# Written order on every engine, and the second read of each batch as float32 products in four column tiles

## The chip, the cores and the metric

The kernel runs on one core of one Trainium2 chip. The metric is the device time of one execution in microseconds (us), as the median of several runs; lower is better. A profile of one execution gives the start and length of every instruction on the five engines: PE (TensorE, the matrix products; its weight loads stand apart as PEld), DVE (VectorE), ACT (ScalarE), POOL (GpSimd) and SP (SyncE, which here only issues DMAs).

## What is computed

```python
# x: 8 batches, 8 heads, 512 tokens, 64; state: 8, 8, 32, 64 (float32)
scores  = scale * x @ state^T            # first read: tokens look at the 32 states
a       = softmax(scores);   xread = a @ state
scores2 = scale * state @ x^T            # second read: the states look at the tokens
a2      = softmax(scores2);  sread = a2 @ x
y = concatenate([xread, sread], axis=2)  # 544 rows of 512 in each batch
h = maximum(y @ w_in, 0)                 # w_in: 512 x 2048
out = (h * h) @ w_out                    # w_out: 2048 x 512
```

The weights arrive as 64-bit floats and are turned into float32 on the chip. Most products are made of float32r halves: each operand is split into a high part (`hi`, a cast) and the rest (`lo`), and three products hi·hi, hi·lo and lo·hi stand for one.

## The kernel before

**Blocks.** The 4352 rows of the output are worked through in nine blocks: block b (0 to 7) holds the 512 token rows of batch b, block 8 the 256 state rows of all batches. In a block the 2048 hidden columns are cut in 16 chunks `fc`. `hidden.b.fc` makes one chunk: 6 products (12 of half the width in block 8) into the PSUM tile `ph`, then relu, square, the cast to `g_hi` and the rest `g_lo`. `accumulate.b.fc` multiplies it with chunk fc of `w_out`: three products for each of the four 128-row tiles `acc`, so 12 (6 in block 8). On PE the chunks stand as hidden.k+1 ahead of accumulate.k, so that the work after the products of chunk k has the time of accumulate.k-1 and hidden.k+1. Blocks 0 and 1 are interleaved in halves (0.0–0.7, 1.0–1.7, 0.8–0.15, 1.8–1.15), since the weights are still arriving: `decode_wi` and `prep_wo` turn them into float32 (one operation on ACT, four on DVE, L353 to L362), `split_wo` splits them. Half of block 0 uses plain float32 products (L644, L685).

**Ahead of each block, for its batch** (`class Attention`, L382): `prep` transposes x into `xT`; `scores` makes both score matrices by products of 64x32 tiles, eight side by side on PE (`by_head`, L337); `transposed_scores`, `softmax` and `split_k` make the first read's weights as `k_hi`, `k_lo`; `make_w2` (L573) multiplies state with `w_in` in the same 64x32 tiles, so that `hidden` needs one product chain (four times per block, w2.b.0 to w2.b.6). For the second read, `exp_s` makes the exponentials `e2` (ACT, L467), `transposes` turns them by PE, and `sread` multiplies them with x: all four heads of a group g at once, of which the diagonal quarter is used. From batch 2 on both operands are split into halves (`split_n`, L513, and L531), which makes 12 products of 128x128 by 256 columns for each g; in batches 0 and 1 it is four float32 products (L540), which PE runs as two instructions each.

**PSUM.** `acc` has four banks, `ph` two, and one tile of two banks (`banks`, L296) is used in turn by scores, w2, transposes and sread: each must be read out in full before the next is written.

**Order.** `PLAN` (L29) lists the steps; a step is a generator, `~name` runs it to its next `yield`, `name` to its end. `keep_order` (L269) ties every instruction to the one before it on its engine while `pinned` holds. At the word `loose` (behind accumulate.0.15) it stops: from there the scheduler of the tile framework orders each engine's instructions, with high priority for the products of `by_head`. Block 8 stands between blocks 6 and 7.

**Who does what.** `SECOND` names the exceptions from the usual engine: `pick(key, first, second)` (L306) takes the second engine for a name listed there. The rests of splits and the two softmax operations on whole tiles (L482, L494) are done on POOL from batch 2 on, and so is `split_wi` (L618) for block 8. Squares: in block 0 and the first half of block 1 by ACT (relu, square, cast: L670, L671, L676); otherwise ACT relu, DVE multiply (L675), ACT cast; then DVE makes `g_lo` (L678).

Of the kernel before, what the change touches and what calls it, by code (L numbers as in the profile page):

```python
# [28 lines left out]
PLAN = """  # L29
# [12 lines left out]
    ~prep_wo.2 ~decode_wi.4 w2.0.1 split_wo.0 ~hidden.0.2 ~prep_wo.2 ~prep_wo.3 ~decode_wi.4 prep_wo.2 ~decode_wi.4
    ~transposes.0.0
    hidden.0.2 ~decode_wi.5 accumulate.0.1 decode_wi.4 transposes.0.0 ~decode_wi.5 load_wo.12 ~prep_wo.3
    ~decode_wi.7 ~decode_wi.5 ~prep_wo.3 decode_wi.5 ~prep_wo.3 ~decode_wi.8 load_wo.13 ~sread.0.0 ~decode_wi.6
    ~split_wo.1 prep_wo.3 split_wo.1 ~hidden.0.3 ~sread.0.0 ~decode_wi.6 ~decode_wi.7 ~decode_wi.6 ~prep_wo.4
    sread.0.0 ~w2.0.2 decode_wi.6
    hidden.0.3 ~prep_wo.4 load_wo.14 accumulate.0.2 ~decode_wi.7 ~prep_wo.4 w2.0.2 ~decode_wi.7 ~decode_wi.9
    ~prep_wo.4 decode_wi.7 prep_wo.4 ~prep_wo.8 load_wo.15 ~decode_wi.8 ~prep.1.0 ~split_wo.2 ~decode_wi.9
    ~decode_wi.8 ~hidden.0.4 split_wo.2 prep.1.0 ~decode_wi.8 ~prep_wo.5 prep.1.1 ~decode_wi.9 decode_wi.8 ~prep.1.2  # L50
    hidden.0.4 ~prep_wo.5 load_raw.10 ~decode_wi.9 accumulate.0.3 prep.1.2 ~prep_wo.5 decode_wi.9 ~prep_wo.9
    prep.1.3 ~prep_wo.5 load_raw.11 ~prep_wo.10 ~prep_wo.8 prep_wo.5 ~prep_wo.8 ~prep_wo.9 ~transposes.0.1
    ~split_wo.3 ~prep_wo.8 ~hidden.0.5 transposes.0.1 split_wo.3 prep_wo.8 ~prep_wo.6 ~prep_wo.9 ~sread.0.1
    ~split_wo.8 ~prep_wo.6 ~prep_wo.9
    hidden.0.5 ~prep_wo.6 split_wo.8 accumulate.0.4 ~sread.0.1 ~prep_wo.6 prep_wo.9 ~decode_wi.10 sread.0.1
    prep_wo.6 start.2 ~split_wo.9 load_p.2.0 ~decode_wi.10 split_wo.9 ~decode_wi.10 ~w2.0.3 ~decode_wi.11
    ~prep_wo.10 load_p.2.1 ~decode_wi.10 ~split_wo.4 ~decode_wi.11 w2.0.3 split_wo.4 scores.1 decode_wi.10
    ~prep_wo.7 load_p.2.2 ~decode_wi.11 ~prep_wo.7 ~hidden.0.6 transposed_scores.1.0 transposed_scores.1.1
# [6 lines left out]
    ~hidden.1.0 ~decode_wi.11 ~accumulate.0.7 ~prep_wo.10 decode_wi.11 transposes.1.0
    hidden.1.0 load_raw.13 ~prep_wo.10 prep.2.0 prep_wo.10 ~sread.1.0 accumulate.0.7 prep.2.1 prep.2.2 prep.2.3
    ~sread.1.0 ~hidden.1.1 ~split_wo.7 sread.1.0 ~w2.1.2 ~hidden.1.1 split_wo.7 accumulate.1.0 ~w2.1.2
    hidden.1.1 ~split_wo.10 w2.1.2 ~hidden.1.2 split_wo.10 ~transposes.1.1 ~hidden.1.2 accumulate.1.1 transposes.1.1
    hidden.1.2 ~decode_wi.12 ~decode_wi.13 ~decode_wi.12 ~sread.1.1 ~decode_wi.12 ~prep_wo.11 ~decode_wi.13
    ~decode_wi.12 ~decode_wi.13 ~hidden.1.3 ~sread.1.1 decode_wi.12 ~decode_wi.13 load_raw.14 ~prep_wo.12 sread.1.1  # L70
    accumulate.1.2 decode_wi.13 ~hidden.1.3 ~prep_wo.11 load_raw.15 ~prep_wo.12 ~prep_wo.11 ~prep_wo.12 ~prep_wo.13
    ~prep_wo.11 ~w2.0.4
    hidden.1.3 prep_wo.11 ~hidden.1.4 ~w2.0.4 ~prep_wo.12 ~prep_wo.13 ~split_wo.11 w2.0.4 accumulate.1.3 ~hidden.1.4
    split_wo.11 prep_wo.12 ~decode_wi.14
    hidden.1.4 ~hidden.1.5 ~split_wo.12 ~decode_wi.14 ~prep_wo.13 split_wo.12 ~hidden.1.5 accumulate.1.4
    ~decode_wi.14 ~prep_wo.13 ~decode_wi.14 prep_wo.13 ~decode_wi.15
    hidden.1.5 ~split_wo.13 ~hidden.1.6 decode_wi.14 ~decode_wi.15 split_wo.13 ~hidden.1.6 accumulate.1.5
    ~decode_wi.15 ~decode_wi.15 decode_wi.15 ~prep_wo.14
    hidden.1.6 ~prep_wo.15 ~prep_wo.14 ~hidden.1.7 ~prep_wo.14 ~prep_wo.15 ~prep_wo.14 ~hidden.1.7 accumulate.1.6
    ~prep_wo.15 prep_wo.14 ~prep_wo.15 ~split_wo.14 prep_wo.15  # L80
    hidden.1.7 ~split_wo.15 ~w2.0.6 split_wo.14 split_wo.15 ~hidden.0.8 ~w2.0.6 w2.0.6 ~hidden.0.8 ~accumulate.1.7
# [4 lines left out]
    hidden.0.12 ~hidden.0.13 ~hidden.0.13 accumulate.0.12
    hidden.0.13 ~hidden.0.14 ~hidden.0.14 accumulate.0.13
    hidden.0.14 ~hidden.0.15 ~hidden.0.15 accumulate.0.14
    hidden.0.15 accumulate.0.15 loose
    hidden.1.8 scores.2 load_n.2.0  # L90
    hidden.1.9 accumulate.1.8 transposed_scores.2.0 exp_s.2.0 w2.1.6
    hidden.1.10 accumulate.1.9 transposed_scores.2.1 exp_s.2.1 softmax.2.0
    hidden.1.11 accumulate.1.10 softmax.2.1 split_n.2.0 load_states.5
    hidden.1.12 accumulate.1.11 transposes.2.0 sread.2.0 split_n.2.1 prep_states.5
    hidden.1.13 accumulate.1.12 transposes.2.1 start.3 load_p.3.0 load_p.3.1 load_p.3.2 load_p.3.3 load_part.1
    hidden.1.14 accumulate.1.13 w2.2.0
    hidden.1.15 accumulate.1.14 sread.2.1
    hidden.2.0 accumulate.1.15 prep.3.0
    hidden.2.1 accumulate.2.0 prep.3.1 load_n.3.0 w2.2.2
    hidden.2.2 accumulate.2.1 prep.3.2  # L100
    hidden.2.3 accumulate.2.2 prep.3.3
    hidden.2.4 accumulate.2.3 scores.3
    hidden.2.5 accumulate.2.4 transposed_scores.3.0 exp_s.3.0 w2.2.4
    hidden.2.6 accumulate.2.5 transposed_scores.3.1 exp_s.3.1 softmax.3.0
    hidden.2.7 accumulate.2.6 softmax.3.1 split_n.3.0
    hidden.2.8 accumulate.2.7 transposes.3.0
    hidden.2.9 accumulate.2.8 sread.3.0 split_n.3.1 w2.2.6
    hidden.2.10 accumulate.2.9 transposes.3.1
    hidden.2.11 accumulate.2.10 sread.3.1
# [765 lines left out]
```

## Time and profile before

| what | value |
|---|---|
| time, median of 3 runs | 699.42 us (699.08 to 699.65) |
| the profiled execution | 697.38 us |
| its span in the profile | 695.6 us |
| granted PE clock, mean of the span | 0.989 |
| busy: PE, DVE, ACT, POOL | 670.2, 384.6, 322.8, 89.0 us |
| first product of hidden.0.0 | 24.4 us after the start of the span |
| first product of hidden.1.0 | 78.0 us |
| block 8 on PE | 576 to 622 us |
| last product | 691.4 us |

The time of a run holds the span and some 2 us around it. The span is the time from the first to the last instruction; the parts of the profile (busy times, waits, the chain of work that ended last, the timeline) are all of the one profiled execution. A product's own length in the profile (about 390 ns for 512 columns) includes its way through the array, so that the rate of PE is read from the distance between the starts of products.

### The profile page before, as it was taken

How to read it: one execution, taken by the hardware profiler on the slowest of the kernel's cores; microseconds unless marked ns; L12 is line 12 of the kernel's file. 1: busy time of each engine (PE TensorE's matmuls, PEld its weight loads, DVE VectorE, ACT ScalarE, POOL GpSimd, SP SyncE). 2: the span in 40 equal slices, each digit the busy share in tenths (PEclk: the TensorE clock that was granted, in tenths of full speed). 3: DMA queues.
4: the chain of work that ended last, by engine and by line, in shares of the span. 5: the costliest groups of instructions: out<-in, count | busy, mean ns of one | idle time of the engine just before them, and what ended most of it. 6: DMA issues, size and time to landing. Idle time of an engine off the chain costs nothing.

```text
span 695.6 us, 9267 instructions
## 1 busy us (share of the span) xinstructions
PE 670.2 (96%) x3488; PEld 505.9 (73%) x3488; DVE 384.6 (55%) x715; ACT 322.8 (46%) x607; POOL 89.0 (13%) x62
## 2 busy tenths in 40 slices
PE   3599899999999999999999999999999999999997
PEld 2254477768777877787777777778778778987886
DVE  4999979456467345734574445734473434235333
ACT  4476577563435334534453434543463444423322
POOL 0000000032104010401032100410050112400000
PEclk9799999999999999999999999999999999999999
DMA  9975154404231023102310232020010001001001
GB/s 284 394 235 125 50 161 90 132 1 133 60 97 25 1 61 61 61 0 61 62 61 0 61 52 71 0 49 13 1 60 5 12 15 61 1 1 32 0 1 60
DMA packets 84300, 46.21 MB, mean 66 GB/s; under 512 B 65056, under 2 KB 71712, under 8 KB 84256
## 3 DMA queue, kind: packets, MB, share of 16 engines
q1 hardware_dynamic: 82176, 45.10, 23.7%
q10 hardware_dynamic: 2080, 0.52, 0.4%
q8 instruction: 27, 0.44, 0.3%
q14 instruction: 17, 0.14, 0.1%
HBM read 34.08 MB, written 11.01 MB: 65 GB/s over the span
## 4 chain that ended last, share of the span: by engine, by line
PE 90%; DVE 7%; SPq 1%; issue 1%; DMA 1%; ACT 0%; DVEq 0%
PE acc L333 51%; PE ph L333 27%; PE w2ps L341 4%; PE pr L333 2%; PE acc L685 2%; PE ph L644 1%; PE pt L523 1%; PE sc L341 1%; PE pr L540 1%; DMA std<-in_state_dram 1%; DVE wi L362 1%; SPq L560 0%; DVE dec L359 0%; DVE deco L359 0%; DVE deco L362 0%
## 5 line engine op out<-in xcount | busy, mean ns | idle before, releaser
L333 PE MATMUL acc<-wo,g_hi 128*128 128x512 f32 x1024 | 288.8, 394 | 0.0
L333 PEld LDWEIGHTS acc<-wo,g_hi 128*128 128x128 f32 x1024 | 187.2, 188 | 57.6 <-ACT r L674 17.6
L675 DVE SCALAR_TENSOR_TENSOR ph<-ph,r 128x512 f32<-128x512 f32 (+1 forms) x120 | 79.5, 663 | 179.1 <-ACT r L674 179.1
L333 PE MATMUL ph<-k_hi,w 128*128 128x512 f32 x480 | 169.0, 393 | 2.1 <-DVE w L602 1.3
L333 PE MATMUL acc<-wo,g_lo 128*128 128x512 f32 x512 | 168.3, 392 | 0.0
L674 ACT ACTIVATE r<-ph 128x512 f32<-128x512 f32 (+1 forms) x120 | 68.3, 569 | 208.0 <-PE ph L333 207.9
L678 DVE TENSOR_TENSOR g_lo<-ph,g_hi 128x512 fp32r<-128x512 f32 (+1 forms) x136 | 89.2, 656 | 70.0 <-ACT g_hi L676 66.1
L333 PEld LDWEIGHTS acc<-wo,g_lo 128*128 128x128 f32 x512 | 95.6, 188 | 25.7 <-DVE s L492 3.4
L333 PEld LDWEIGHTS ph<-k_hi,w 128*128 128x128 f32 x480 | 90.4, 189 | 24.5 <-issue 2.5
L676 ACT CAST g_hi<-ph 128x512 fp32r<-128x512 f32 (+1 forms) x136 | 76.4, 562 | 66.0 <-DVE ph L675 65.1
L333 PE MATMUL ph<-k_lo,w 128*128 128x512 f32 x240 | 93.9, 391 | 0.0
L311 POOL TENSOR_TENSOR xs<-xn,xs 128x1024 fp32r<-128x1024 f32 x12 | 28.8, 2400 | 425.1 <-ACT xs L310 425.1
L333 PEld LDWEIGHTS ph<-k_lo,w 128*128 128x128 f32 x240 | 45.2, 188 | 9.1
L602 DVE TENSOR_TENSOR w<-w2ps,w 128x512 fp32r<-128x512 f32 x60 | 38.4, 682 | 8.2 <-ACT w L599 8.1
L341 PE MATMUL w2ps<-wi,stT 64*32 64x512 f32 (+1 forms) x544 | 36.8, 583 | 0.5 <-DVE wi L362 0.5
L599 ACT CAST w<-w2ps 128x512 fp32r<-128x512 f32 x60 | 32.4, 596 | 4.2 <-PE w2ps L341 4.2
L685 PE MATMUL acc<-deco,gf 128*128 128x512 f32 x64 | 29.2, 599 | 0.0
L311 POOL TENSOR_TENSOR s<-wi,s 128x1024 fp32r<-128x1024 f32 x8 | 19.2, 2403 | 73.6 <-ACT s L310 73.6
L548 ACT ACTIVATE srd<-pr,r 32x64 f32<-32x64 f32 x64 | 19.4, 304 | 16.0 <-PE pr L333 10.2
L644 PE MATMUL ph<-kf,w 128*128 128x512 f32 x32 | 17.3, 675 | 8.9 <-DVE kf L500 8.3
L333 PE MATMUL ph<-sr_k_hi,s 128*128 128x256 f32 x128 | 25.4, 282 | 0.0
L685 PEld LDWEIGHTS acc<-deco,gf 128*128 128x128 f32 x64 | 12.1, 195 | 13.5 <-issue 13.0
(79 smaller groups left out, 546.7 us busy)
## 6 DMA issues: line engine op xcount, KB each, us to landing
...
```

What stands on the lines that cost most here:

```text
L311: pick(key, PL, V).tensor_sub(lo, src, hi.bitcast(F32))
L333: m = T.matmul(ps, l, r, start=first and i == 0, stop=last and i == len(seq) - 1)
L341: m = T.matmul(ps, l, r, start=True, stop=True)
L548: A.mul(srd[q].rearrange("p e d -> p (e d)"), pr[q, j], r2[q])
L599: A.copy(w[:, u, g, 0], ps[g])
L602: V.tensor_sub(w[:, u, g, 1], ps[g], w[:, u, g, 0].bitcast(F32))
L644: T.matmul(ph, w[c][:, cs], k[c], start=c == 0, stop=c == G - 1)
L674: A.activation(r, ph, AF.Relu)
L675: V.scalar_tensor_tensor(ph, ph, 0.0, r, ALU.max, ALU.mult)
L676: A.copy(ghi, ph)
L678: V.tensor_sub(glo, ph, ghi.bitcast(F32))
L685: T.matmul(acc[i], ghi[:, ts(i, P)], wo[fc], start=first, stop=last)
```

## The change

Four things are changed.

1. `loose` goes, and with it `pinned`, the priorities and the pins in `mm3` and `by_head`: every engine keeps the written order to the end. The steady blocks 2 to 6 come from one template `BLOCK` (b is the block, n the batch behind it, whose attention is made meanwhile). Block 8 is last (`READS`), after block 7. The order of the first two blocks (`FIRST`) is written anew too: among others decode_wi.10 and 11, prep_wo.8 to 10 and split_wo.8 and 9 are later, and both groups of the transposes stand together.
2. `sread` makes one float32 product per head, group of 128 tokens and g: weights of 128x32, 64 columns, the four heads j into the four 32-row quarters of the output. `transposes` does both g at once, `split_n` and the split of the transposed exponentials go.
3. What POOL did in splits and softmax goes to DVE (`pick` has its engines swapped, `SECOND` loses those lists). Nearly all squares are made on ACT; the others (x.3, x.10, x.12 to x.15 and block 8) stay split between ACT and DVE.
4. The scaling of the second read is one ACT operation per g, in place of four; block 8 is stored with one DMA per tile, in place of four.

```diff
-    hidden.0.7 accumulate.0.6 exp_s.1.1 ~softmax.1.0 ~softmax.1.1 ~softmax.1.0 ~split_k.0.0 ~softmax.1.1
...
-    hidden.3.4 accumulate.3.3 scores.4
-    hidden.3.5 accumulate.3.4 transposed_scores.4.0 exp_s.4.0 w2.3.4
-    hidden.3.6 accumulate.3.5 transposed_scores.4.1 exp_s.4.1 softmax.4.0
...
+    hidden.0.6 ~softmax.1.0 ~softmax.1.1 ~exp_s.1.1 ~softmax.1.0 split_wo.4 ~softmax.1.1 exp_s.1.1 ~softmax.1.0
+    ~prep_wo.7 ~softmax.1.1 ~w2.1.0 ~split_wo.5 ~softmax.1.0 ~hidden.0.7 ~w2.1.0 ~softmax.1.1 ~prep_wo.6
+    ~softmax.1.1 ~softmax.1.0 ~prep_wo.6
+    hidden.0.7 softmax.1.0 ~softmax.1.1 ~split_k.0.0 prep_wo.6 ~softmax.1.1 split_k.0.0 accumulate.0.6 ~split_k.0.1
+    softmax.1.1 split_k.0.1 w2.1.0 ~prep_wo.7 ~transposes.1 ~split_wo.6 split_wo.5 ~prep_wo.7 ~hidden.1.0
...
+BLOCK = """
...
+    hidden.{b}.3 accumulate.{b}.2 scores.{n} ~hidden.{b}.4 ~hidden.{b}.4 transposed_scores.{n}.0
+    hidden.{b}.4 transposed_scores.{n}.1 ~exp_s.{n}.0 ~exp_s.{n}.1 accumulate.{b}.3 ~hidden.{b}.5 ~hidden.{b}.5
+    ~exp_s.{n}.0 ~exp_s.{n}.1 ~softmax.{n}.0
+    hidden.{b}.5 ~softmax.{n}.1 exp_s.{n}.0 exp_s.{n}.1 ~softmax.{n}.0 accumulate.{b}.4 ~w2.{b}.4 ~hidden.{b}.6
+    load_states.{s} start.{m} load_p.{m}.0 load_p.{m}.1 load_p.{m}.2 load_p.{m}.3 ~hidden.{b}.6 ~w2.{b}.4
+    ~softmax.{n}.0
...
+    hidden.{b}.10 softmax.{n}.1 accumulate.{b}.9 ~transposes.{n} ~hidden.{b}.11 ~hidden.{b}.11 transposes.{n}
+    hidden.{b}.11 accumulate.{b}.10 ~hidden.{b}.12 ~sread.{n} ~hidden.{b}.12 ~sread.{n}
+    hidden.{b}.12 sread.{n} prep_states.{s} accumulate.{b}.11 ~hidden.{b}.13 ~hidden.{b}.13
...
+    hidden.8.15 accumulate.8.14 accumulate.8.15
...
-            if i.engine in last and pinned[0]:
+            if i.engine in last:
...
     def split(hi, lo, src, key):
         A.copy(hi, src)
-        pick(key, PL, V).tensor_sub(lo, src, hi.bitcast(F32))
...
+        yield
+        pick(key, V, PL).tensor_sub(lo, src, hi.bitcast(F32))
...
-        def transposes(self, g):
-            b, e2 = self.b, self.e2.pop(g)
-            pt = banks(f"pt{b}_{g}")[:, 0].rearrange("p (k q) -> p k q", k=KC)
...
+        def transposes(self):
             b = self.b
+            t = banks(f"pt{b}")
+            for g in range(G):
+                e2 = self.e2.pop(g)
+                for k in range(KC):
+                    T.transpose(t[:, g, ts(k, P)], e2[:, k], ident)
+            yield
...
+                eT = p2.tile([P, G, S], F32, tag="wraw", name=f"eT{b}", bufs=RB)
+                evac(f"eT.{b}", eT, t)
...
-                hi, lo = self.xs.pop(g)
-                mm3(pr, [((eT[:, 0, k], eT[:, 1, k]), (hi[:, k], lo[:, k])) for k in range(KC)])
...
+            for g in range(G):
                 for k in range(KC):
+                    for j in range(NC):
+                        q = slice(32 * j, 32 * j + 32)
+                        xh = self.xn[:, k, 2 * j + g] if b < NX else self.xn[:, 2 * j + g, k]
+                        e = self.eT[g][:, P * k + 32 * j : P * k + 32 * j + 32]
+                        T.matmul(pr[q, g], e, xh, start=k == 0, stop=k == KC - 1)
+            yield
+            srd = p2.tile([P, G, D], F32, tag="srd", name=f"srd{b}", bufs=1)
+            for g in range(G):
+                A.mul(srd[:, g], pr[:, g], self.r2[g])
...
-                for j in range(4):
-                    SP.dma_start(out_v[4 * i + j, S : S + Ns], o[32 * j : 32 * j + 32])
+                pick(f"store.{i}", SP, A).dma_start(out_v[4 * i : 4 * i + 4, S : S + Ns], o)
```

More of the change, by code (lines that the diff above doesn't have):

```diff
@@ L42 @@
[L42 to L58, printed above, removed]
@@ L65 @@
[L65 to L81, printed above, removed]
@@ L82 @@
-    hidden.0.8 accumulate.1.7 load_states.2 ~hidden.0.9 ~hidden.0.9 accumulate.0.8
-    hidden.0.9 prep_states.2 ~hidden.0.10 load_part.0 ~hidden.0.10 accumulate.0.9
+    load_raw.6 ~prep.0.2 ~decode_wi.1 load_raw.7 prep.0.2 ~decode_wi.1 load_wo.5 ~prep.0.3 load_wo.6 ~prep_wo.0
+    decode_wi.1 load_wo.7 prep.0.3 ~prep_wo.0 ~w2.0.0 load_raw.8 ~prep_wo.0 load_raw.9 scores.0 w2.0.0 ~prep_wo.0
+    load_wo.8 load_wo.9 ~decode_wi.2 prep_wo.0 transposed_scores.0.0 ~decode_wi.3 transposed_scores.0.1 ~softmax.0.0
@@ new lines @@
+    start.1 ~prep_wo.1 load_n.1.0 ~softmax.0.1 ~softmax.0.0 load_n.1.1 ~softmax.0.1 ~softmax.0.0 ~exp_s.0.0
+    ~prep_wo.2 load_n.1.2 ~softmax.0.1 ~softmax.0.0 ~exp_s.0.0 ~softmax.0.1 load_n.1.3 ~softmax.0.0 ~decode_wi.4
+    ~softmax.0.1 ~softmax.0.0 ~softmax.0.1 softmax.0.0 softmax.0.1 exp_s.0.0 ~hidden.0.0 ~decode_wi.2 ~exp_s.0.1
+    ~decode_wi.2 ~exp_s.0.1 ~decode_wi.3 ~hidden.0.1 ~decode_wi.2
+    hidden.0.0 exp_s.0.1 decode_wi.2
+    hidden.0.1 accumulate.0.0 ~decode_wi.3 load_wo.10 ~prep_wo.1 ~decode_wi.3 ~decode_wi.5 ~prep_wo.1 decode_wi.3
@@ new lines @@
+    ~prep_wo.1 ~decode_wi.6 load_wo.11 ~prep_wo.2 ~w2.0.1 ~split_wo.0 prep_wo.1 w2.0.1 split_wo.0 ~prep_wo.2
+    ~hidden.0.2 ~prep_wo.3 ~decode_wi.4 ~prep_wo.2 ~decode_wi.4 ~transposes.0
+    hidden.0.2 prep_wo.2 ~decode_wi.4 accumulate.0.1 transposes.0 ~decode_wi.5 decode_wi.4 ~decode_wi.5 ~decode_wi.7
+    load_wo.12 ~prep_wo.3 ~decode_wi.5 ~prep_wo.3 decode_wi.5 ~sread.0 ~split_wo.1 ~prep_wo.3 load_wo.13
+    ~decode_wi.8 ~hidden.0.3 split_wo.1 ~sread.0 prep_wo.3 ~prep_wo.4 sread.0 ~prep_wo.4 ~w2.0.2 start.2
@@ new lines @@
+    hidden.0.3 load_p.2.0 ~decode_wi.6 accumulate.0.2 ~prep_wo.4 ~decode_wi.6 w2.0.2 ~prep_wo.4 load_p.2.1
+    ~decode_wi.6 prep_wo.4 decode_wi.6 load_p.2.2 ~prep.1.0 ~decode_wi.7 ~split_wo.2 ~decode_wi.8 ~decode_wi.9
+    split_wo.2 ~hidden.0.4 prep.1.0 ~decode_wi.7 ~decode_wi.8 load_p.2.3 ~decode_wi.7 ~prep_wo.5 prep.1.1 ~prep.1.2
+    ~decode_wi.8
+    hidden.0.4 decode_wi.7 accumulate.0.3 load_wo.14 ~prep_wo.5 prep.1.2 load_wo.15 decode_wi.8 ~prep_wo.5
+    ~prep_wo.8 load_raw.10 prep.1.3 ~decode_wi.9 ~prep_wo.9 ~prep_wo.5 ~decode_wi.9 ~w2.0.3 prep_wo.5 ~split_wo.3
@@ new lines @@
+    ~decode_wi.9 ~hidden.0.5 w2.0.3 split_wo.3 decode_wi.9 ~prep_wo.6 scores.1 ~prep_wo.8
+    hidden.0.5 load_raw.11 ~prep_wo.6 ~prep_wo.8 accumulate.0.4 transposed_scores.1.0 ~prep_wo.10
+    transposed_scores.1.1 ~exp_s.1.0 ~softmax.1.0 ~exp_s.1.0 ~softmax.1.1 ~hidden.0.6 ~split_wo.4 exp_s.1.0
+    ~softmax.1.0 ~exp_s.1.1 ~softmax.1.0 accumulate.0.5
+    hidden.0.6 ~softmax.1.0 ~softmax.1.1 ~exp_s.1.1 ~softmax.1.0 split_wo.4 ~softmax.1.1 exp_s.1.1 ~softmax.1.0
+    ~prep_wo.7 ~softmax.1.1 ~w2.1.0 ~split_wo.5 ~softmax.1.0 ~hidden.0.7 ~w2.1.0 ~softmax.1.1 ~prep_wo.6
@@ new lines @@
+    ~softmax.1.1 ~softmax.1.0 ~prep_wo.6
+    hidden.0.7 softmax.1.0 ~softmax.1.1 ~split_k.0.0 prep_wo.6 ~softmax.1.1 split_k.0.0 accumulate.0.6 ~split_k.0.1
+    softmax.1.1 split_k.0.1 w2.1.0 ~prep_wo.7 ~transposes.1 ~split_wo.6 split_wo.5 ~prep_wo.7 ~hidden.1.0
+    transposes.1 split_wo.6 ~prep_wo.7 ~sread.1 ~hidden.1.0 ~prep_wo.8 prep_wo.7 prep_wo.8 ~accumulate.0.7 ~sread.1
+    hidden.1.0 ~split_wo.8 sread.1 split_wo.8 load_n.2.0 ~prep_wo.9 ~decode_wi.10 ~prep_wo.10 ~decode_wi.10
+    ~prep_wo.9 ~w2.1.2 accumulate.0.7 ~decode_wi.10 ~prep_wo.9 ~decode_wi.10 prep_wo.9 ~w2.1.2 ~hidden.1.1
@@ new lines @@
+    decode_wi.10 ~prep_wo.10 load_raw.12 ~split_wo.7 w2.1.2 accumulate.1.0 ~hidden.1.1 split_wo.7 ~prep_wo.10
+    ~split_wo.9
+    hidden.1.1 ~hidden.1.2 split_wo.9 prep_wo.10 ~decode_wi.11 accumulate.1.1 prep.2.0 ~hidden.1.2 ~decode_wi.11
+    prep.2.1 ~decode_wi.11 ~split_wo.10
+    hidden.1.2 ~hidden.1.3 ~decode_wi.11 split_wo.10 ~hidden.1.3 accumulate.1.2 decode_wi.11 prep.2.2 load_raw.13
+    prep.2.3 ~decode_wi.12
+    hidden.1.3 start.3 load_p.3.0 ~prep_wo.11 ~w2.0.4 ~decode_wi.12 ~prep_wo.12 ~prep_wo.11 ~hidden.1.4
@@ new lines @@
+    ~decode_wi.12 ~w2.0.4 ~prep_wo.11 load_p.3.1 ~decode_wi.12 ~hidden.1.4 accumulate.1.3 w2.0.4 load_p.3.2
+    decode_wi.12
+    hidden.1.4 ~decode_wi.13 ~prep_wo.11 ~hidden.1.5 load_raw.14 ~decode_wi.13 prep_wo.11 load_p.3.3 ~hidden.1.5
+    accumulate.1.4 ~decode_wi.13 ~prep_wo.12 ~decode_wi.13 ~prep_wo.12 ~split_wo.11
+    hidden.1.5 decode_wi.13 ~hidden.1.6 split_wo.11 load_raw.15 ~prep_wo.12 ~decode_wi.14 accumulate.1.5 ~hidden.1.6
+    prep_wo.12 ~decode_wi.14 ~decode_wi.14 ~decode_wi.14 ~split_wo.12
@@ new lines @@
+    hidden.1.6 ~hidden.1.7 split_wo.12 decode_wi.14 ~decode_wi.15 accumulate.1.6 ~hidden.1.7 ~decode_wi.15
+    ~decode_wi.15 ~decode_wi.15 decode_wi.15 ~prep_wo.13 ~hidden.0.8
+    hidden.1.7 ~prep_wo.14 ~prep_wo.13 ~prep_wo.15 ~prep_wo.14 ~w2.0.6 ~hidden.0.8 ~prep_wo.13 ~prep_wo.14
+    ~accumulate.1.7 ~prep_wo.13 ~prep_wo.14 ~w2.0.6
+    hidden.0.8 prep_wo.13 w2.0.6 accumulate.1.7 prep_wo.14 ~prep_wo.15 ~prep_wo.15 ~split_wo.13 load_states.2
+    ~hidden.0.9 ~prep_wo.15 ~split_wo.14 split_wo.13 ~hidden.0.9 accumulate.0.8 split_wo.14 prep_wo.15 ~split_wo.15
@@ L84 @@
+    hidden.0.9 prep_states.2 ~hidden.0.10 split_wo.15 load_part.0 ~hidden.0.10 accumulate.0.9
     hidden.0.10 ~hidden.0.11 ~hidden.0.11 accumulate.0.10
     hidden.0.11 ~w2.1.4 ~hidden.0.12 ~w2.1.4 w2.1.4 ~hidden.0.12 accumulate.0.11
[L86 to L109, printed above, removed]
@@ L132 @@
-    hidden.4.2 accumulate.4.1 prep.5.2
-    hidden.4.3 accumulate.4.2 prep.5.3
-    hidden.4.4 accumulate.4.3 scores.5
-    hidden.4.5 accumulate.4.4 transposed_scores.5.0 exp_s.5.0 w2.4.4
-    hidden.4.6 accumulate.4.5 transposed_scores.5.1 exp_s.5.1 softmax.5.0
-    hidden.4.7 accumulate.4.6 softmax.5.1 split_n.5.0
-    hidden.4.8 accumulate.4.7 transposes.5.0
-    hidden.4.9 accumulate.4.8 sread.5.0 split_n.5.1 w2.4.6
-    hidden.4.10 accumulate.4.9 transposes.5.1
-    hidden.4.11 accumulate.4.10 sread.5.1
@@ L164 @@
-    hidden.6.2 accumulate.6.1 prep.7.2
-    hidden.6.3 accumulate.6.2 prep.7.3
-    hidden.6.4 accumulate.6.3 scores.7
-    hidden.6.5 accumulate.6.4 transposed_scores.7.0 exp_s.7.0 w2.6.4
-    hidden.6.6 accumulate.6.5 transposed_scores.7.1 exp_s.7.1 softmax.7.0
-    hidden.6.7 accumulate.6.6 softmax.7.1 split_n.7.0
-    hidden.6.8 accumulate.6.7 transposes.7.0
-    hidden.6.9 accumulate.6.8 sread.7.0 split_n.7.1 w2.6.6
-    hidden.6.10 accumulate.6.9 transposes.7.1
-    hidden.6.11 accumulate.6.10 sread.7.1
@@ L332, in mm3 @@
         for i, (l, r) in enumerate(seq):
-            m = T.matmul(ps, l, r, start=first and i == 0, stop=last and i == len(seq) - 1)
-            if pin and not pinned[0]:
-                tc.keep_in_program_order(m)
+            T.matmul(ps, l, r, start=first and i == 0, stop=last and i == len(seq) - 1)
     def by_head(jobs):
-        for i, (ps, l, r) in enumerate(jobs):
-            with tc.high_priority() if i and not pinned[0] else nullcontext():
-                m = T.matmul(ps, l, r, start=True, stop=True)
-            if i and not pinned[0]:
-                tc.keep_in_program_order(m)
+        for ps, l, r in jobs:
+            T.matmul(ps, l, r, start=True, stop=True)
     def decode(raw, shape, nm, out=None, tag="dec"):
@@ L679, in hidden, with accumulate @@
         return ghi, glo
-    def accumulate(acc, fc, g, nt, first, last, pin):
+    def accumulate(acc, fc, g, nt, first, last):
         ghi, glo = g
@@ L698, in store @@
         for i in range(nt // P):
-            if add is not None:
-                o = add[i]
+            o = p2.tile([P, DM], F32, tag="o", name=f"o{blk}_{i}", bufs=OB) if add is None else add[i]
+            if add is None:
+                evac(f"out.{blk}.{i}", o, acc[i])
+            else:
                 V.tensor_add(o, acc[i], o)
-            else:
-                o = p2.tile([P, DM], F32, tag="o", name=f"o{blk}_{i}", bufs=OB)
-                evac(f"out.{blk}.{i}", o, acc[i])
             if blk < B:
```

254 lines of the change are left out of this document (99 added, 155 removed).

## The prediction

> **What bounds the kernel now.** I read the page first: who is busy, at which clock, and which engine the chain of work that ended last runs through.
>
> ```profile
> span 695.6 us, 9267 instructions
> PE 670.2 (96%) x3488; PEld 505.9 (73%) x3488; DVE 384.6 (55%) x715; ACT 322.8 (46%) x607; POOL 89.0 (13%) x62
> ...
> PEclk9799999999999999999999999999999999999999
> ...
> PE 90%; DVE 7%; SPq 1%; issue 1%; DMA 1%; ACT 0%; DVEq 0%
> ```
>
> PE is busy for 96% of the span at nearly full clock, and 90% of the chain is PE. Busy is not yet dense, so the next views are the busy times by stretch, and the chain and timeline in a steady block.
>
> ```profile
> 24.43:62.50 38.07, 37.54 (x136) 18.51 (x136) 36.37 (x81) 24.66 (x48) 0.00 (x0) 0.94 0.77 249
> 62.50:82.00 19.50, 15.93 (x80) 6.75 (x80) 19.28 (x44) 11.79 (x23) 0.00 (x0) 0.95 0.33 68
> 82.00:104.00 22.00, 22.00 (x103) 15.95 (x101) 17.68 (x35) 15.65 (x32) 0.00 (x0) 0.97 0.53 140
> 104.00:131.00 27.00, 27.00 (x141) 20.66 (x141) 22.95 (x42) 19.02 (x34) 0.00 (x0) 1.00 0.41 104
> ...
> 430.00:506.00 76.00, 76.00 (x403) 58.35 (x401) 39.57 (x71) 34.12 (x63) 13.91 (x9) 1.00 0.10 29
> ```
>
> Columns: stretch, its length, then busy time of PE, weight loads, DVE, ACT and POOL. Up to 82 us DVE never rests (36.4 of 38.1, 19.3 of 19.5) and PE has holes; from 82 us on PE has none. In a steady block (430 to 506) DVE and ACT each work about half of the time. How dense PE is there, the chain tells, with start and length of each piece:
>
> ```profile
> 449.39 0.44 PE pt L523 x4
> 449.83 2.77 PE acc L333 x12
> 452.60 1.36 PE ph L333 x6
> 453.96 1.07 PE pr L333 x9
> 455.04 2.75 PE acc L333 x12
> 457.78 1.36 PE ph L333 x6
> 459.14 0.35 PE pr L333 x3
> ```
>
> Six products take 1.36 and twelve 2.72 to 2.77, so 227 ns each, back to back. In steady state time is saved only by taking work from PE, and every new wait of PE is paid in full.
>
> **The read that goes and the read that comes.** One old read of a group g costs 1.07 + 0.35 = 1.42, and the next accumulation 2.75 in place of 2.72: 1.45, so 2.9 us a batch for both groups. In batches 0 and 1 the chain has the float32 form, and below it stand the 64x32 tiles, whose float32 instructions run side by side:
>
> ```profile
> 40.69 1.74 PE pr L540 x8
> ```
> ```profile
> 429.03 0.39 PE L333 MATMUL ph<-k_hi,w 128*128 128x512 f32 x1
> ...
> 430.48 1.09 PE L341 MATMUL sc<-xT,stT 64*32 64x512 f32 x16
> 431.50 1.65 PE L333 MATMUL acc<-wo,g_hi 128*128 128x512 f32 x6
> 432.99 0.86 PE L333 MATMUL acc<-wo,g_lo 128*128 128x512 f32 x3
> ```
>
> Float32 over 256 columns takes 1.74 / 8 = 217 ns an instruction, the transposes' 128 columns 0.44 / 4 = 110; so 64 columns should take 55. The old form costs 2 x 1.74 = 3.5 us a batch. The sixteen instructions of scores on eight tiles take 1.02 (430.48 to 431.50): two rounds of 512 columns, each 2 x 217 = 0.43, so 0.86 of streaming. The switch of tile shape costs the rest: 0.16 there, 0.09 before (429.03 + 1.36 = 430.39, not 430.48) and 0.13 behind (six products take 1.49, not 1.36), together about 0.39.
>
> The new read has 2 groups x 4 k x 4 heads = 32 products, 64 instructions, 16 on each of four tiles. Side by side that is 16 x 0.055 = 0.88, plus 0.39: **1.27 us**. No row has a 128x32 tile. The bounds are 0.88 (switch free) and, all four tiles one after another, 64 x 0.055 + 0.39 = 3.9. I take 1.27, by the row it is nearest to: the 64x32 tiles differ only in that two row halves share the array.
>
> - Batches 2 to 7: 6 x (2.9 - 1.27) = -9.8.
> - Batches 0 and 1: 2 x (3.5 - 1.27) = -4.4.
> - The transposes of both groups share one entry: 0.44 + 0.05 behind them twice becomes 0.44 + 0.39 + 0.05, or 0.1 less: 6 x 0.1 = -0.6.
>
> The weight loads have to hide behind the products:
>
> ```profile
> 411.64 0.18 PEld L341 LDWEIGHTS w2ps<-wi,stT 64*32 64x32 f32 x16 [0.35 <-issue]
> ```
> ```profile
> L341 PEld LDWEIGHTS w2ps<-wi,stT 64*32 64x32 f32 x544 | 6.4, 105 | 15.0 <-issue 9.6 <-ACT wo L314 1.5 <-DVE wi L362 1.4
> ```
>
> A load takes 105 ns, yet sixteen, two for each tile, are done in 0.18, while the first products of 0.43 run: they overlap. The Trainium skill, "TensorE: Matmul & The Clock Gate", in "Part 3: Packing small matmuls — row/col tiling", says that a weight load overlaps running products only when its row group differs; four 128x32 tiles share all rows, so this speaks against the change. The trace does not bear it out strictly, since the second load for each tile was made while that very tile's first product ran. It returns below as a rival.
>
> **The start.** Waits of PE (those up to 24 us, for the first loads and the first softmax, are untouched and left out):
>
> ```profile
> PE sc L341 <- ACT w L326: 1.5, 1, 1.5
> PE ph L333 <- DVE w L602: 1.3, 1, 1.3
> PE ph L333 <- ACT w L599: 0.7, 1, 0.7
> PE ph L644 <- ACT w L326: 0.5, 1, 0.5
> PE w2ps L341 <- DVE wi L362: 0.5, 1, 0.5
> ```
>
> Together 4.5 us, and behind nearly all stands a full DVE. The new order puts DVE work behind hidden.1.0 that stood before it, priced by these rows:
>
> ```profile
> L362 DVE SCALAR_TENSOR_TENSOR deco<-wo_raw,deco 128x512 uint32<-128x512 uint32 x16 | 10.9, 683 | 0.1
> ...
> L316 DVE TENSOR_TENSOR wo<-deco,wo 128x512 fp32r<-128x512 f32 x16 | 10.9, 684 | 0.0
> ...
> L357 DVE TENSOR_SCALAR deco<-deco 128x512 uint32<-128x512 uint32 x16 | 6.7, 422 | 0.1
> ```
> A whole decode is 2 x 0.42 + 2 x 0.68 = 2.2. Later are decode_wi.10, prep_wo.9 (2.2 each), the last two operations of prep_wo.8 (1.4), two short ones each of decode_wi.11 and prep_wo.7 (0.8 each), one of prep_wo.10 (0.4), and three split_wo (2.1): 9.9 us. The holes of 4.5 can close. But the work comes back between hidden.1.0 and hidden.0.10, where DVE had 22.0 - 17.7 + 27.0 - 23.0 = 8.3 us free (82 to 131): it is nearly full there too, and some wait must come back. Bounds 0 and -4.5; I take **-3.0**.
>
> **The new wait.** I walked the template's order through one block with the trace's durations. Every use of the shared two-bank tile finds it free in time but one: w2.b.4 takes it from scores, whose last readers are the two exponentials on ACT, now written behind the relu, square and cast of hidden.b.5.
>
> ```profile
> 106.84 0.58 ACT L670 ACTIVATE ph<-ph 128x512 f32<-128x512 f32 x1
> 107.45 0.58 ACT L671 ACTIVATE ph<-ph 128x512 f32<-128x512 f32 x1
> 108.07 0.59 ACT L676 CAST g_hi<-ph 128x512 fp32r<-128x512 f32 x1
> ```
> ```profile
> 68.82 0.68 ACT L467 ACTIVATE e<-sc,nb 128x512 f32<-128x512 f32 x1
> 69.39 0.20 ACT L467 ACTIVATION_READ_ACCUMULATOR e<-sc,nb 128x1 f32 x1
> ```
> ```profile
> 685.94 0.39 PE L333 MATMUL ph<-k_hi,w 128*128 128x512 f32 x1
> ...
> 686.43 0.60 ACT L674 ACTIVATE r<-ph 128x512 f32<-128x512 f32 x1 [2.13 <-PE ph L333]
> ```
>
> Count from the end of scores on PE. hidden.4 (0.13 + 1.36), accumulate.3 (2.72) and hidden.5 (1.36) are through at 5.57; the last product ends 0.16 later and ACT starts 0.10 after that (686.33 to 686.43): 5.83. Relu, square and cast take 1.82 (106.84 to 108.66): 7.65. Two exponentials take 0.57 + 0.20 + 0.68 = 1.45: 9.10, and 0.1 for the hand-over: 9.2. PE has finished accumulate.4 at 8.29 and would switch at 8.38. It waits **0.8 us** in each of blocks 2 to 6: +4.1. Behind w2.b.4 stands all of PE. Bounds: 0, if the tile is free sooner, and 1.6, if ACT comes as late again.
>
> **What I cost at nothing.** POOL's work moves to DVE (two softmax operations and a rest for each g, 6 x 0.68 = 4.1 a batch), but ten squares of 0.7 leave DVE: still about half of the block. ACT gains ten operations of 0.58 and loses the two long casts of `split_n`. The chain behind a hidden chunk stays near 2.6 us (three on ACT, 1.82, then 0.7 on DVE) against accumulate and hidden, 2.72 + 1.36 = 4.08, as cover; without cover it would cost what it is late, 16 times a block. Copying both transposes takes ACT one operation of about 1.0; walked like the wait above, it ends 0.9 us before the read needs it. SP's loads stand half a block ahead of use. Block 8 moves as a whole, at the same cost. At the end its last chain (four operations on half the columns) has one accumulation of 1.36 as cover, where block 7 had 2.72: up to 1 us; with some edges at block changes I take **+0.5**.
>
> **Sum.** -9.8 - 4.4 - 0.6 - 3.0 + 4.1 + 0.5 = -13.2. The span goes from 695.6 to 682.4. The profiled execution took 697.4, 2.0 below the median of 699.4; the difference is set against the median: **686.2 us**.
>
> **The rivals.**
>
> - *Loads not hidden.* If each round waits for its load (105 ns) as well, a read costs 16 x (0.105 + 0.055) + 0.39 = 2.95, 1.68 more; eight reads add 13.4: 699.6, no change. This is how the skill's rule of row groups would act here. Against it: the sixteen loads in 0.18.
> - *One tile after another* (slower). If the four column tiles do not run side by side, as would also follow if the change did not place them apart, a read costs 3.9, and eight add 21: 707.3. It decides from a read of 1.27 + 13.2 / 8 = 2.9 us on. For it: no row has full-height narrow tiles; against it: the row of scores, where four column tiles of each half do run together.
> - *More waits of the written order.* The scheduler could put something else first; a fixed order cannot. If ACT is 1 us late at one more place in each of six blocks (the copy of the transposes has 0.9 to spare): 692.
> - *No wait at w2.b.4.* Then 682.1. Against it: the walk above, which uses nothing but rows.
>
> **How the numbers follow.** Forecast 0.62 (own range 682.5 to 690, by the start's bounds and half of the unknown wait), more waits 0.13, no wait 0.10, loads not hidden 0.09, one after another 0.06. From 680.5 to 694.5 holds all but the last two (0.15) and the ends of the others (about 0.05). A measurement here tells about 0.2%, 1.4 us, from no change. Faster is forecast, more waits and no wait: 0.84, a trifle off for the worst of the waits; loads not hidden lies on the line: same 0.06; slower 0.10.
>
> **What would show it.** In the profile after: `pr` rows of 128x32 with about 0.9 to 1.1 us from first start to the next product (right), 2.5 or 3.5 (a rival). PE waits on ACT at w2 of about 0.8, five times. hidden.1.0 before 76 us, not 78. POOL near 0, DVE over 0.9 busy up to some 120 us. A period of a block of about 74.6, not 75.5. Wrong it would be by a `pr` that takes 3 us, or by PE holes at other steps in each block.

## The result, and the profile after

The changed kernel takes 692.33 us (median of 4 runs, 691.66 to 692.75), the kernel before beside it 699.46: ratio 0.9898, 95% interval 0.9881 to 0.9915. It is faster by 7.1 us where 13.2 were forecast. Its profiled execution took 692.39 us and has a span of 690.6, 5.0 less than before; the profiled execution of before lay 2 us below its median. One run of those reported below, 839.79 us at a granted clock of 0.749 where the nine others of its kernel (POOL's rests, in "DVE in the start") had 0.986 to 0.996, is left out of that kernel's median.

The page of the changed kernel, with busy times of the engines:

```profile
span 690.6 us, 9688 instructions
...
PE 655.5 (95%) x3824; PEld 488.1 (71%) x3824; DVE 363.4 (53%) x671; ACT 331.6 (48%) x609; POOL 0.7 (0%) x6
...
PEclk9999999999999999999999999999999999999998
```

PE has 15 us less to do, yet its share falls from 96 to 95%: two thirds of what was taken from PE did not come off the span. The timeline of PE shows the new read in a steady block:

```profile
248.26 0.39 PE L280 MATMUL ph<-k_hi,w 128*128 128x512 f32 x1
248.58 1.10 PE L483 MATMUL pr<-xn,eT 128*32 128x64 f32 x64
249.61 0.73 PE L280 MATMUL acc<-wo,g_hi 128*128 128x512 f32 x2
```

PE runs the 32 products as 64 instructions, and all 64 are through in 1.03 us (248.58 to 249.61). With 0.09 before (the product ahead ends its 0.23 at 248.26 + 0.23 = 248.49) and 0.13 behind (two products in 0.58, not 0.45, at 250.19) a read costs 1.25 us; 1.27 was forecast. So the expected gain is there, and the loss is elsewhere. Three places in time divide the span: the first product of hidden.0.10, the last product, the end.

Before, in PE's timeline:

```profile
131.04 0.39 PE L333 MATMUL ph<-k_hi,w 128*128 128x512 f32 x1
```

After, in the same view:

```profile
124.82 0.39 PE L280 MATMUL ph<-k_hi,w 128*128 128x512 f32 x1
...
680.34 0.40 PE L280 MATMUL acc<-wo,g_lo 128*128 128x512 f32 x1
```

The busy times of the last stretch, from the last product to the end (length, then PE, weight loads, DVE, ACT, POOL, clock, DMA share, GB/s), before:

```profile
691.39:695.60 4.21, 0.39 (x2) 0.00 (x0) 0.69 (x1) 0.34 (x1) 0.00 (x0) 0.86 0.64 237
```

and after:

```profile
680.34:690.60 10.26, 0.40 (x2) 0.00 (x0) 0.69 (x1) 0.33 (x1) 0.00 (x0) 0.68 0.17 51
```

| stretch | before | after | difference | forecast |
|---|---|---|---|---|
| to hidden.0.10 | 131.0 | 124.8 | -6.2 | -7.4 |
| to the last product | 560.4 | 555.5 | -4.8 | -6.3 |
| to the end | 4.2 | 10.3 | +6.1 | +0.5, with the last chain |

The last product comes 11 us earlier than before; 6 of them are given back after it, while only the last copies and stores run. Over this stretch the DMAs move 51 GB/s in the mean, for two stores of 256 KB; before it was 237, for four. The waits of PE after:

```profile
PE w2ps L285 <- ACT e L409: 2.7, 5, 0.5
PE acc L618 <- DVE deco L304: 2.4, 2, 1.8
PE pr L483 <- ACT eT L273: 1.1, 1, 1.1
PE w2ps L285 <- DVE wi L304: 0.7, 1, 0.7
```

The first is the forecast wait of w2.b.4, five times. The third was not forecast. Of these places the experiments asked.

### The profile page after: what moved, and what is told of

It is laid out like the page before. It is cut to its first block, busy times and chain, and to the rows that moved or that the text cites. A ratio compares the mean times of both kernels' runs of the same rounds, so it can differ in the third digit from the quotient of the medians.

```text
span 690.6 us, 9688 instructions
## 1 busy us (share of the span) xinstructions
PE 655.5 (95%) x3824; PEld 488.1 (71%) x3824; DVE 363.4 (53%) x671; ACT 331.6 (48%) x609; POOL 0.7 (0%) x6
## 4 chain that ended last, share of the span: by engine, by line
PE 84%; DVE 6%; ACT 3%; DMA 2%; SPq 2%; issue 1%; DVEq 0%; ACTq 0%
PE acc L280 45%; PE ph L280 26%; PE w2ps L285 4%; PE acc L618 4%; PE ph L584 2%; PE sc L285 1%; DMA wi_raw<-in_moe_w_in_dram 1%; PE pr L483 1%; PE pt L461 1%; ACT e L409 1%; SPq L352 1%; DMA std<-in_state_dram 1%; ACT ph L604 1%; ACT g_hi L609 1%; DVE deco L304 1%
## 5 line engine op out<-in xcount | busy, mean ns | idle before, releaser
L280 PE MATMUL acc<-wo,g_hi 128*128 128x512 f32 x1024 | 317.2, 391 | 0.4 <-DVE o L635 0.4
L280 PEld LDWEIGHTS acc<-wo,g_hi 128*128 128x128 f32 x1024 | 190.6, 188 | 41.2 <-ACT ph L603 0.8
L280 PE MATMUL acc<-wo,g_lo 128*128 128x512 f32 x512 | 199.6, 390 | 0.3 <-DVE g_lo L611 0.3
L280 PE MATMUL ph<-k_hi,w 128*128 128x512 f32 x480 | 172.2, 399 | 0.0
L603 ACT ACTIVATE ph<-ph 128x512 f32<-128x512 f32 x84 | 48.9, 582 | 164.9 <-PE ph L280 164.8
L608 DVE SCALAR_TENSOR_TENSOR ph<-ph,r 128x512 f32<-128x512 f32 (+1 forms) x52 | 32.1, 617 | 73.4 <-ACT r L607 73.4
L607 ACT ACTIVATE r<-ph 128x512 f32<-128x512 f32 (+1 forms) x52 | 27.7, 532 | 82.3 <-PE ph L280 82.3
L604 ACT ACTIVATE ph<-ph 128x512 f32<-128x512 f32 x84 | 48.9, 582 | 2.6
L618 PEld LDWEIGHTS acc<-deco,gf 128*128 128x128 f32 x64 | 11.7, 190 | 17.1 <-issue 13.2
L280 PEld LDWEIGHTS ph<-sr_k_hi,s 128*128 128x128 f32 x128 | 21.0, 191 | 0.7
```

The costliest lines, as they stand in the source:

```text
L280: T.matmul(ps, l, r, start=first and i == 0, stop=last and i == len(seq) - 1)
L603: A.activation(ph, ph, AF.Relu)
L604: A.activation(ph, ph, AF.Square)
L607: A.activation(r, ph, AF.Relu)
L608: V.scalar_tensor_tensor(ph, ph, 0.0, r, ALU.max, ALU.mult)
L618: T.matmul(acc[i], ghi[:, ts(i, P)], wo[fc], start=first, stop=last)
```

## The experiments

The median of the kernel before was between 697.3 and 699.5 from one set of runs to the next, so a kernel is compared with the one beside it, and the ratios with each other. The changed kernel itself, run again as a mark:

> The changed kernel once more, unedited, as the mark for the runs beside it: in the same relation to the kernel before as measured first, 0.990, since the tail of 10.3 us and the five waits at w2.b.4 are fixed by the order.

692.23 us, beside 698.24: 0.9914 (0.9898 to 0.9931), as at first within the intervals, and the span is again 690.6.

### The tail: eight stores in place of two

```diff
-                pick(f"store.{i}", SP, A).dma_start(out_v[4 * i : 4 * i + 4, S : S + Ns], o)
+                for j in range(4):
+                    SP.dma_start(out_v[4 * i + j, S : S + Ns], o[32 * j : 32 * j + 32])
```

> The kernel after with one edit: block 8's two result tiles are stored with four DMAs of 32 rows each, as before. Theory (a store whose destination is four pieces of 32 rows is spread over 4 of the 16 DMA engines, and as it is now the last thing, it stands in the open): the time from the last product to the end falls from 10.3 us back to about 4.2, so 692.3 becomes about 686.3. Rival (block 8 last is slow to store whatever the DMA's shape): no change, 692.

688.59 beside 697.31, ratio 0.987 (0.9852 to 0.9887). The stretch after the last product:

```profile
681.05:687.33 6.28, 0.40 (x2) 0.00 (x0) 0.69 (x1) 0.32 (x1) 0.00 (x0) 0.92 0.33 84
```

6.3 us, not 10.3, and not 4.2: only two thirds of the forecast. SP's timeline says why:

```profile
681.40 3.64 SPq L640 DMA_DIRECT2D out_dram<-o  x8
```

SP issues for 3.6 us, one store after the other, against 2.5 us for four stores before. So the stores are the cause, and this cure has a price of its own. In the whole time the gain is smaller: the ratio lies 0.0028 to 0.0044 below the two of the unedited kernel, 2 to 3 us, and in this execution the last product stands 0.7 later (681.05 for 680.34).

### The tail: the same two stores into one piece

```diff
-                pick(f"store.{i}", SP, A).dma_start(out_v[4 * i : 4 * i + 4, S : S + Ns], o)
+                SP.dma_start(out_v[i, ts(0, P)], o)
```

> The kernel after with one edit: each of block 8's two tiles is stored with one DMA to 128 rows in one piece (the first rows of batches 0 and 1), in place of four pieces of 32 rows, so block 8's rows land in a wrong place and its own are not written. Theory (the shape of the destination decides how many of the 16 DMA engines a store uses): the time from the last product to the end falls from 10.3 to about 4.2 us, the time by 6 against the unedited kernel beside it. Rival (being last, or two DMAs of 256 KB at the end, is what costs): no change.

This kernel leaves block 8's own rows unwritten. 686.48 beside the unedited 692.23, 5.75 less; ratio 0.9832 (0.9817 to 0.9846). Length of the last stretch, and the stores in the view of DMA issues (KB each, us to landing):

```profile
680.48:684.73 4.25, 0.39 (x2) 0.00 (x0) 0.69 (x1) 0.32 (x1) 0.00 (x0) 1.00 0.33 123
```
```profile
out_dram<-o SPq DMA_DIRECT2D x2, 256.0 KB, 2.0
```

As many stores, as many bytes, the same place at the end: only the destination differs, and 4.25 us are back at what they were. It is neither block 8 at the end nor the size of the stores. How many of the 16 DMA engines carry a store shows in the trace. Beside the packets of 2048 bytes there are some of 4 bytes: 8 among the 264 packets of the two stores of the changed kernel, 32 among the 288 of these two. Read as one for each engine that takes part, that is 4 engines for a store and 16. The busy share of the 16 engines agrees (in tenths, 40 slices), first of the changed kernel from 679 to 691 us, then of this one from 679 to 685:

```profile
DMA  0000000000251301222222222222222210000000
```
```profile
DMA  0000000000000000029999379997000000000000
```

The Trainium skill, "DMA: Bandwidth & Descriptors", in "Why a DMA increments its semaphore by 16 and not by 1", says that a DMA is spread over the largest number up to 16 that divides the slowest dimension of both sides. By that rule 4 x 32 rows go to 4 engines and 128 rows to 16; the trace agrees with both.

### The tail: two queues

```diff
-                pick(f"store.{i}", SP, A).dma_start(out_v[4 * i : 4 * i + 4, S : S + Ns], o)
+                for j in range(4):
+                    (SP, A)[i].dma_start(out_v[4 * i + j, S : S + Ns], o[32 * j : 32 * j + 32])
```

> The kernel after with one edit: block 8's tiles are stored with four DMAs of 32 rows each, tile 0's issued by SP and tile 1's by ACT. With all eight on SP the tail was 6.3 us, of which SP issued for 3.7. Theory (issuing one after another is what is left of the tail): four and four, 1.5 to 1.8 us less, a tail of about 4.6. Rival (the DMA engines are the limit there): 6.3 as with SP alone.

687.61, 4.6 less than the unedited kernel beside it; ratio 0.9851 (0.9836 to 0.9865).

```profile
680.04:685.39 5.35, 0.39 (x2) 0.00 (x0) 0.69 (x1) 0.33 (x1) 0.00 (x0) 0.91 0.37 98
```

5.35, 0.9 less than with SP alone, where 1.5 to 1.8 was expected: issuing is part of the rest, and four and four don't take it away. ACT's four issues still stand one after the other, 1.90 us in all from 681.19, where the two stores into one piece took SP 1.14. What else is in the 1.1 us between 5.35 and 4.25 stays open.

### The wait at w2.b.4

```diff
-    ... accumulate.{b}.3 ~hidden.{b}.5 ~hidden.{b}.5
-    ~exp_s.{n}.0 ~exp_s.{n}.1 ~softmax.{n}.0
+    ... accumulate.{b}.3 ~hidden.{b}.5
+    ~exp_s.{n}.0 ~exp_s.{n}.1 ~hidden.{b}.5 ~softmax.{n}.0
```

The wait in the changed kernel: ACT's timeline, and then PE's.

```profile
216.08 0.58 ACT L603 ACTIVATE ph<-ph 128x512 f32<-128x512 f32 x1 [2.29 <-PE ph L280]
...
217.31 0.59 ACT L609 CAST g_hi<-ph 128x512 fp32r<-128x512 f32 x1
217.79 0.69 ACT L409 ACTIVATE e<-sc,nb 128x512 f32<-128x512 f32 x1
...
218.47 0.69 ACT L409 ACTIVATE e<-sc,nb 128x512 f32<-128x512 f32 x1
```
```profile
218.38 0.39 PE L280 MATMUL acc<-wo,g_lo 128*128 128x512 f32 x1
219.30 1.09 PE L285 MATMUL w2ps<-wi,stT 64*32 64x512 f32 x16 [0.53 <-ACT e L409]
```

Both exponentials stand behind the square of hidden.2.5 on ACT, the second ends at 219.16, and PE goes on at 219.30, 0.5 late.

> The kernel after with one edit: in blocks 2 to 6 the two exponentials of the second read stand ahead of the relu, square and cast of hidden.b.5 on ACT. Theory (w2.b.4 waits for them, 0.5 to 0.6 us in each block): the wait goes, the period of a block falls from 74.35 to about 73.8, the time by 2.7 to about 689.6. Rival (the wait moves to accumulate.b.5, whose chunk now comes 1.5 us later): no change, 692.

689.23, ratio 0.9884 (0.9867 to 0.9902): the interval overlaps that of the unedited kernel, so the times alone don't tell. The trace does. The waits on `e` are gone from the list of PE's waits, no other came in their place, and from scores to scores a block takes 73.73 us (284.33 to 358.06), where the unedited kernel takes 74.35 (283.63 to 357.98). Five times 0.62 is 3.1; of it 1.4 is hidden in this execution, since scores.2 stood at 140.35 and not at 138.98, long before the edit takes hold. The first 140 us differ by that much between executions: with the same order up to there, scores.2 stood at 139.72 with the eight stores, at 139.12 with the stores into one piece and at 138.71 with the two queues.

### What the narrow tiles give

```diff
-                for k in range(KC):
-                    for j in range(NC):
+                for j in range(NC):
+                    for k in range(KC):
```

> The kernel after with one edit: in the second read the loops are turned, all four products of a head one after another, then the next head; the same 32 products. Theory (PE hands out products in order and one tile's products block those behind them): the read takes 64 x 0.055 = 3.5 us in place of 1.03, eight times 2.5 more: about 712. Rival (each column tile works off its own products and later ones overtake): the read stays between 1.0 and 1.4, 692 to 695.

701.09 in one run, its span 699.3. PE's timeline:

```profile
250.69 2.41 PE L483 MATMUL pr<-xn,eT 128*32 128x64 f32 x64
253.03 0.73 PE L280 MATMUL acc<-wo,g_hi 128*128 128x512 f32 x2
```

2.34 us in place of 1.03: between the two theories. A tile's products do hold up the products behind them, but not all: 64 x 0.055 would be 3.5. So tiles run fully side by side where the order hands them out in turn, and only in part otherwise. Eight reads of 1.31 more are 10.5 us; the span grew by 8.7 with the same late stores. A steady block takes 1.30 more (75.65 for 74.35), but the two reads in the start hardly show: scores.2 stands at 139.81, for 138.98.

### The read alone in the kernel before

```diff
-                hi, lo = self.xs.pop(g)
-                mm3(pr, [((eT[:, 0, k], eT[:, 1, k]), (hi[:, k], lo[:, k])) for k in range(KC)])
+            for i in range(KC * NC):
+                k, j = divmod(i, NC)
...
+                with tc.high_priority() if i and not pinned[0] else nullcontext():
+                    m = T.matmul(pr[q], eT[:, k, q], xh, start=k == 0, stop=k == KC - 1)
```

> The kernel before with the new read alone: float32 products in four column tiles for each g by itself, kept together as the products of scores are, no splits of its operands; order, squares, POOL's other work, block 8's place and stores as before. By the terms of the prediction, two entries of 0.39 and 2 x 0.44: 1.66 a batch. Theory (PE-bound, each us off PE is a us): six batches 1.24 less, two 1.84 less, at most -11, or 688.4; 690 to 692 if the full DVE takes back what the first two give. Rival (the scheduler tears the products apart and pays more switches): 696 or more.

690.57, ratio 0.990 (0.9881 to 0.992): 6.7 us less than before, not 11. The read by itself is worth as much as the whole change. A part of what it does not give stands in PE's waits, and in the chain of a steady block:

```profile
PE acc L333 <- ACT g_hi L670: 1.7, 2, 0.9
```
```profile
421.83 1.10 PE sc L341 x16
...
424.18 2.47 DVE xT L438 x4
426.65 0.57 DVE o L324
427.22 0.59 DVE m L480
427.81 0.60 DVE o L324
428.41 0.07 DVE nb L463
...
428.51 0.78 ACT e L467 x2
...
429.81 0.48 ACT g_hi L670
...
430.33 3.09 PE acc L333 x12
```

The free scheduler put four transposes of the next batch, two copies and a reduction on DVE ahead of the small operation `nb` that an exponential waits for, and this exponential ahead of a hidden chunk's cast: PE loses 1.25 us in such a block (24 products in 6.70, from 426.56 to 433.26, not in 5.45). There are two such blocks, so this is 2.5 of the 4.3 us that are missing; the rest was not traced. Here the free order has a wait that the written one doesn't have.

### DVE in the start

```diff
+    w_out_lo: 0 1 2 3 4 5 6 7 8 9 10 11 12 13 14 15
```

> The kernel after with one edit: the rests of the splits of w_out (16 operations, 0.68 each on DVE, all in the first 125 us) are made by POOL. Theory (the waits of PE up to 125 us stand behind a full DVE): 10.9 us less on DVE there, and the waits on decoded w_out and w_in (2.4 + 0.7) and the late pieces of accumulate (about 0.5) go: 2 to 3.5 us less than the unedited kernel beside it. Rival (the order holds DVE up, not its load, or POOL's 1.3 us apiece come late): within 1 us of it.

695.62 (nine runs, 694.63 to 698.50), 3.4 *more* than the unedited kernel beside it; ratio 0.9972 (0.9958 to 0.9987), for 0.9914. Both theories miss. The groups on DVE from 25 to 125 us, first of the changed kernel, then of this one, whose lines are one further:

```profile
L304 DVE SCALAR_TENSOR_TENSOR wi<-wi_raw,dec 128x512 uint32<-128x512 uint32 x14 | 9.6, 684 | 0.0
```
```profile
L305 DVE SCALAR_TENSOR_TENSOR wi<-wi_raw,dec 128x512 uint32<-128x512 uint32 x14 | 13.5, 966 | 0.1
```

The same fourteen operations take 966 ns in the mean in place of 684. Looked at one by one, ten take 0.67 to 0.69 us, and the four that meet a POOL operation 1.52 to 1.79, nearly as long as the two one after the other:

```profile
108.96 0.69 DVE L612 TENSOR_TENSOR g_lo<-ph,g_hi 128x512 fp32r<-128x512 f32 x1 [0.26 <-ACT g_hi L610]
109.57 1.79 DVE L305 SCALAR_TENSOR_TENSOR wi<-wi_raw,dec 128x512 uint32<-128x512 uint32 x1
```
```profile
109.52 1.29 POOL L268 TENSOR_TENSOR wo<-deco,wo 128x512 fp32r<-128x512 f32 x1 [13.20 <-ACT wo L266]
```

DVE's operation starts at 109.57, POOL's runs until 110.81, and DVE's ends at 111.36, 0.55 later: it waited. Most of the work that left DVE came back as blocked time: from 25.75 to 124.82 us DVE is busy for 91.3 us, only 2.5 less than in the changed kernel (93.9), though fourteen operations, 9.5 us, are gone from it. PE's wait for `g_lo`, which DVE makes, grows from 0.3 to 2.2; that this and not the order makes the kernel slower is likely, but was not tried apart. Whether the start is bound by DVE's load was not settled by this run; the next pair speaks to it.

### The three mends together, and one step of the start

The edits are those of the two queues and of the exponentials, and:

```diff
-    ... transposes.2 ~sread.2 load_part.1 ~hidden.1.9 ~sread.2 sread.2
+    ... transposes.2 load_part.1 ~hidden.1.9 ~sread.2 ~sread.2 sread.2
```

> The kernel after with three edits: block 8's stores by four DMAs of 32 rows for each tile, one tile on SP, one on ACT (alone: 4.6 less than the unedited kernel); the exponentials ahead of hidden.b.5 on ACT (alone: the five waits of 0.5 gone); and hidden.1.9 between transposes.2 and sread.2 on PE, so that the copy of the transposes (PE waited 1.1 for it) has a cover. Theory (three separate losses on PE's own path, which add): 4.6 + 2.5 + 1.1 = 8.2 less than the unedited kernel's 692.2, about 684, ratio 0.98 to before. Rival (they share a bound behind them): less than 6.

683.55 us (5 runs) beside 698.01: ratio 0.9788 (0.9774 to 0.9801). Against the unedited kernel's 0.9914 that is 1.3% or 8.8 us (7.7 against the 0.9898 measured first); 8.2 were expected, so the three losses add. The unforeseen wait, in the chain of the changed kernel,

```profile
157.90 0.89 PE pt L461 x8
158.78 0.02 issue
158.81 1.02 ACT eT L273
159.83 0.04 issue
159.87 1.10 PE pr L483 x64
```

is, with hidden.1.9 between, covered:

```profile
159.53 0.87 PE pt L461 x8
160.40 1.38 PE ph L280 x6
161.78 1.03 PE pr L483 x64
```

The second kernel has in addition:

```diff
-    hidden.0.7 softmax.1.0 ~softmax.1.1 ~split_k.0.0 prep_wo.6 ~softmax.1.1 split_k.0.0 accumulate.0.6 ...
+    hidden.0.7 prep_wo.6 softmax.1.0 ~softmax.1.1 ~split_k.0.0 ~softmax.1.1 split_k.0.0 accumulate.0.6 ...
```

> As e7_three_mends, and in the first batches the last operation of prep_wo.6 on DVE stands ahead of the last one of softmax.1.0. Theory (accumulate.0.6 waits 1.8 us for that operation, while DVE itself waits 0.3 for ACT beside it; the operations of softmax.1 come 0.4 later, and hidden.1.0 had 1.2 to spare): 0.5 to 1 us less than e7_three_mends. Rival (DVE is full, what is gained here is lost at hidden.1.0): the same within 0.3.

682.71, ratio 0.9779 (0.9764 to 0.9795): 0.8 less, as expected, but the intervals overlap. In the list of PE's waits the one on `deco` falls from 2.4 to 1.0, and a new one of 1.0, `pt` on DVE's `w`, appears; the one on `wi` grows from 0.7 to 1.1. So a part at least moved on, as DVE's full time in the start would have it; whether 0.8 us remain is open.

## Why the prediction was right, and where it failed

The mechanism was right for the read and for the wait at w2.b.4. That the time still lies near 692 is in part luck: it misses the forecast's own range (682.5 to 690) and stands where the rival of more waits had it, but it got there mostly by the stores at the end, which no term of the sum and no rival held.

1. **PE as the bound, and the cost of the new read: right.** 1.25 us measured, 1.27 forecast, 2.9 and 3.5 taken away. Both rivals against it (loads not hidden, 2.95; one tile after another, 3.9) fell. The loop turned around is neither of them: with the tiles one after another in the order, the 64 instructions took 2.34, not the 3.5 of tiles that never overlap. The period of a steady block, 74.35, is a little under the forecast 74.6.
2. **The start: 1.2 us too much was hoped for** (-6.2 for -7.4), in this execution. With the same order hidden.0.10 began between 124.54 (the two queues) and 126.18 (the exponentials moved): the size differs by execution, but all lie behind the forecast's 123.6. hidden.0.0 began 1.3 us later than before here (25.75 for 24.43), but that isn't the reason: with the stores into one piece it began at 24.74, and hidden.0.10 still at 124.93. Between the two PE's holes closed only from 4.1 to 3.0 us (the fifth wait of the prediction's 4.5, 0.5 on `wi`, lies before 24 us): the old waits went, and waits of 2.4 on `deco` came in their place, so more came back than the forecast's 1.5. hidden.1.0 came at 77.1, not before 76.
3. **The new wait at w2.b.4: the right place, five times, too dear** (4.1 forecast; 2.7 in the list of waits, 3.1 by the period of a block, which is what its going is worth). In the sum ACT started 0.10 behind the last product; here it was 0.03 (215.66 + 0.39 to 216.08), and from there to the end of the second exponential it took 3.08 (216.08 to 219.16), not 3.27. Moved, the wait was gone.
4. **The walk missed one wait** of 1.1 at sread.2. It went through the template, where accumulate.{b}.10 stands between the transposes and the read. In the order of the first blocks the products of accumulate.0.15 stand ahead of both (`~accumulate.0.15` issues them; the word behind the transposes only stores), so nothing covers the copy. The rival of more waits was this, in a single place and not in every block.
5. **The step that failed is the end.** The prediction said that block 8 moves as a whole, at the same cost, and gave +0.5 for its last chain. It did not cost the stores, though the change names them: one DMA for each tile in place of four. The end grew by 6.05 us. With its stores into one piece the kernel is 5.75 faster, nearly the 6.1 between forecast and result (692.3 for 686.2). Not everything else came out, though. By the spans the miss is 8.2 (690.6 for 682.4), of which by the table 1.2 and 1.5 lie ahead of the end. The time misses by 2 less, because the forecast added the 2.0 by which the profiled execution of before lay below its median, and the changed kernel's lies at its median: this too is luck. Earlier, this store stood ahead of block 7's 70 us, and no wait of PE shows it; the move to the end took its cover away and the new shape made it slow. By the tails the move alone costs 2 (6.3 for 4.2, with block 8's old stores at the end); the new shape alone, with block 8 in its old place, was not run.
6. **Where the gain comes from.** The read alone gives the whole of 1.0%. Order, squares (ACT alone makes them in 84 of the 136 chunks of split products, for 16 before, so not in nearly all), POOL's work and the place of block 8 together gain about 0.5% when the stores are mended (0.9851 for 0.990), and lose it again as the change has them. What each of them gives for itself was not tried.

The kernel with the three mends beats both, with 0.9788.
